# A scan with state followed by an MLP: a new order table, arithmetic taken off GpSimd, and loads issued by two queues

## The chip, the cores and the metric

One core of a Trainium2 chip runs the whole program. The time is microseconds on the device, from one launch, median of three runs.

## The reference, cut to what matters

```python
B, H, S, D = 4, 8, 768, 40                       # r, k, v, w, a, b: [B, H, S, D], float32
state = zeros((B, H, D, D))
for t in range(S):
    y[:, :, t] = einsum('bhd,bhde->bhe', r_t, state)
    Sa = einsum('bhde,bhe->bhd', state, a_t)
    state = state * w_t[:, :, None, :] - einsum('bhd,bhe->bhde', Sa, b_t)
    state = state + einsum('bhd,bhe->bhde', v_t, k_t)
x = y.transpose(0, 2, 1, 3).reshape(3072, 320)
h = x @ w_in                                     # 320 -> 2048
g = h * erf(softplus(h))
out = g @ w_out                                  # 2048 -> 320
```

The state of each of 32 heads is a 40 x 40 matrix that 768 steps of time update one after the other. The MLP needs x, the outputs of all heads of a time step.

## The kernel before, in words

The scan is done in chunks of 32 time steps. Two groups (g) of 16 heads each are gone through one after the other, each in 6 stages of 128 steps, so there are 12 stages (q = 0 to 11) of 4 chunks (c). `build` (L1074) writes the operations of all stages down in program order. Five parts make a stage:

- `prep` (L618): loads w, and builds decay products over the stage by scans on VectorE (scanS L632, scanP L636).
- `aphase` (L645), per chunk: loads k, b and a in one transfer (kba, L666), scales them (ab L667, bk L672), multiplies on TensorE into PSUM (A, L677), masks (Am, L684) and writes the lower part to HBM (AD, L686); transposes b (bT, L695).
- `tphase` (L701), once a stage: reads the triangles of all chunks back (Ti, L711; Ap, L714), solves them on VectorE by 14 pairs of small operations (Tm L724, Ts L725), writes the result out and reads it in another layout (TD L727, tb L730), transposes it (R, L733) and completes the inverse on TensorE (W, DAD, L740).
- `chain` (L750), per chunk, the part that is serial over time: loads of v in two layouts (zv, vx), of r (rt), and of r and v side by side (rv, L771, tile vt); then Zm <- state (L778), Z (L785), zt, U (L794), us (L798), the 4 pieces of u put into the tile Vu (L799 to L806: in stage 0 copies from PSUM named zmu, later 4 transfers a chunk named zu), UT (L821), vtu, PQ (L830), PQm (L833), MY (L841, L845), and the new state (MT, L848) and the output (Ym, L852), which goes to HBM (xw, L858) at the end of a stage.
- the MLP, for 8 blocks of 256 tokens by 256 columns a stage: `load_x` (xr, xh L989, xl L990), mm1 in three-part precision (L1006), hc (copy out of PSUM, L1010), the activation built of tanh, ln, exp and gelu on ScalarE (L1014), nd and rho on VectorE (L1039, L1040), then E and G (L1051, L1052) and mm2 (L1061). The weights arrive as 64-bit floats and are converted in the first part of the run (w1 to w6, wlo, wr1; L932 to L963).

Each operation goes through `Plan.add` (L276) with the list of engines that may run it. What runs where and when is not decided there: `Plan.schedule` (L301) takes two tables, `ORDER` (L16), a permutation of all operations in which a negative number means a filler, and `ENGINES` (L202), one letter for each operation in program order (P TensorE, A ScalarE, V VectorE, G GpSimd, S SyncE). The instructions are emitted in the order of the table; each engine, and SyncE as the only issuer of transfers, works through its own in that order and waits in place. A filler (`warm`, L578) is a 512-column bf16 matmul of a constant that nothing reads. If the lengths don't fit the operations, a list scheduler (L314 on) makes an order instead.

`dma` (L575) puts every transfer on SyncE. The tile vt has 104 rows (two halves of heads, at rows 0 to 39 and 64 to 103) of 8 x 128 columns; one transfer of 104 x 4 KB fills it.

Of the kernel before, what the change touches and what calls it, by code (L numbers as in the profile page):

```python
# [1192 lines left out]
```

## Time and profile before

| | us |
|---|---|
| runs | 860.70, 861.12, 871.73 |
| median | 861.12 |
| span of the profiled execution (first to last instruction) | 855.2 |

The profiled execution's own time is not listed apart from its span; the median is 5.9 us above that span. A page of the profile gives busy times of the engines; the chain of waits follows the work that ended last back from the end; stretches are counted from the start of the span.

### The profile page before, as it was taken

To read this page: it belongs to the slowest core of one execution; us is meant where nothing else is said; L and a number is where in the kernel's file an instruction comes from. 1 tells how busy PE (TensorE), PEld (TensorE's weight loads), DVE (VectorE), ACT (ScalarE), POOL (GpSimd) and SP (SyncE) were. 2 spreads that over 40 slices of the span, in tenths; PEclk is the share of its full clock that TensorE was granted. 3 is DMA by queue.
4 is the path that set the end of the run, shared out by engine and by line. 5 is a ranking of instruction groups with operands and counts; after the bars stand their busy time and mean duration, and the time that the engine had idled before them with its cause. 6 is when DMAs were issued, how large, how long until landed. Compare 5 with 4: busy or idle time off the path is not lost.

```text
span 855.2 us, 32264 instructions
## 1 busy us (share of the span) xinstructions
PE 741.9 (87%) x13794; PEld 572.6 (67%) x13794; DVE 626.0 (73%) x1331; ACT 563.6 (66%) x1055; POOL 145.3 (17%) x124
## 2 busy tenths in 40 slices
PE   0596898798889998989888998899899999899987
PEld 0343546667767777767667776687777777677864
DVE  5588776687767787879687887768688766565764
ACT  5156424677756776865875874685685787567993
POOL 0302111102012012033030100231130240112100
PEclk9998998999999999999999999989999999899998
DMA  7756664665675755556645555746546543512100
GB/s 213 216 155 156 172 157 119 134 135 142 135 169 115 145 139 123 138 121 143 160 122 118 139 130 115 158 109 146 141 112 128 126 112 92 123 39 66 36 16 19
DMA packets 185585, 107.58 MB, mean 126 GB/s; under 512 B 134268, under 2 KB 167804, under 8 KB 185436
## 3 DMA queue, kind: packets, MB, share of 16 engines
q1 hardware_dynamic: 185436, 105.46, 51.8%
q8 instruction: 110, 1.80, 0.9%
q14 instruction: 39, 0.32, 0.1%
HBM read 83.72 MB, written 14.16 MB: 114 GB/s over the span
## 4 chain that ended last, share of the span: by engine, by line
PE 43%; DMA 21%; DVE 14%; SPq 8%; ACT 6%; issue 6%; POOL 1%; DVEq 0%; ACTq 0%; POOLq 0%
PE po L1061 15%; PE ph L1006 10%; SPq L576 8%; DMA Zs<-Ab 3%; PE pA L740 3%; DMA Ti<-AD 3%; PE ph L579 3%; DMA Tb<-TD 2%; PE my L841 2%; PE pQ L830 2%; PE pA L677 2%; DMA bk<-in_kba_e 2%; DMA AD<-Zs 2%; DVE h L1052 2%; PE my L794 2%
## 5 line engine op out<-in xcount | busy, mean ns | idle before, releaser
L1061 PE MATMUL po<-wo,h 128*128 128x320 f32 x768 | 255.1, 459 | 6.1 <-DVE h L1052 5.8
L1061 PEld LDWEIGHTS po<-wo,h 128*128 128x128 f32 x768 | 135.7, 195 | 51.4 <-DVE h L1052 8.7
L1014 ACT ACTIVATE l<-l 128x512 f32<-128x512 f32 x192 | 112.0, 625 | 18.2 <-DVE nd L1039 14.4
L1006 PE MATMUL ph<-xh,wih 128*128 128x256 f32 x384 | 96.1, 332 | 3.4 <-ACT h L571 3.4
L1006 PE MATMUL ph<-xh,wil 128*128 128x256 f32 x384 | 78.0, 285 | 0.0
L1006 PE MATMUL ph<-xl,wih 128*128 128x256 f32 x384 | 77.7, 284 | 0.0
L1052 DVE SCALAR_TENSOR_TENSOR h<-l,h 128x512 f32<-128x512 f32 x96 | 70.3, 739 | 3.0 <-POOL l L1051 2.1
L1040 DVE SCALAR_TENSOR_TENSOR r<-nd,r 128x512 f32<-128x512 f32 x96 | 68.1, 709 | 5.9 <-POOL nd L1039 4.8
L1039 POOL TENSOR_TENSOR nd<-l,r 128x512 f32<-128x512 f32 x27 | 35.7, 1321 | 206.9 <-DVE r L1040 120.4
L1006 PEld LDWEIGHTS ph<-xh,wih 128*128 128x128 f32 x384 | 61.3, 194 | 10.2 <-ACT h L571 4.3
L571 ACT COPY Zm<-MT 40x320 f32<-40x320 f32 x71 | 32.4, 457 | 50.5 <-DVE MT L848 45.6
L579 PE MATMUL ph<-d 104*128 104x512 bf16 x257 | 65.7, 407 | 0.0
L1051 POOL TENSOR_TENSOR l<-l,r 128x512 f32<-128x512 f32 x27 | 38.2, 1419 | 158.6 <-ACT l L1014 85.8
L1006 PEld LDWEIGHTS ph<-xh,wil 128*128 128x128 f32 x384 | 60.6, 194 | 3.9 <-issue 3.9
L1014 ACT ACTIVATE l<-h 128x512 f32<-128x512 f32 x96 | 57.2, 628 | 7.2 <-DVE h L573 6.0
L1006 PEld LDWEIGHTS ph<-xl,wih 128*128 128x128 f32 x384 | 60.2, 192 | 0.0
L1039 DVE TENSOR_TENSOR nd<-l,r 128x512 f32<-128x512 f32 x69 | 49.7, 721 | 11.6 <-ACT r L1014 9.5
L1006 PE MATMUL ph<-xl,wir 128*128 128x256 f32 x192 | 54.9, 286 | 3.8 <-issue 3.7
L841 PE MATMUL my<-Vu,sg 64*40 64x72 f32 x1536 | 48.5, 233 | 8.7 <-DVE h L1052 3.1
L1014 ACT ACTIVATE r<-r 128x512 f32<-128x512 f32 x96 | 55.2, 624 | 0.4
L1014 ACT ACTIVATE r<-l 128x512 f32<-128x512 f32 x96 | 54.2, 619 | 1.5 <-DVE l L1051 1.4
L1006 PE MATMUL ph<-xh,wir 128*128 128x256 f32 x192 | 54.8, 285 | 0.0
(137 smaller groups left out, 1472.5 us busy)
## 6 DMA issues: line engine op xcount, KB each, us to landing
vt<-in_rv_e SPq DMA_DIRECT2D x48, 416.0 KB
bk<-in_kba_e SPq DMA_DIRECT2D x45, 416.0 KB
wo<-in_moe_w_in SPq DMA_DIRECT2D x10, 512.0 KB
h<-in_moe_w_out SPq DMA_DIRECT2D x10, 512.0 KB
Pr<-in_w_e SPq DMA_DIRECT2D x12, 419.7 KB
Rt<-in_r_e SPq DMA_DIRECT2D x48, 104.0 KB
Vu<-in_v_x SPq DMA_DIRECT2D x96, 40.0 KB
Zm<-in_v_s SPq DMA_DIRECT2D x48, 80.0 KB
```

Source lines behind the costliest of these rows:

```text
L571: self.nc.scalar.copy(o, i)
L576: self.P.add(name, "SP", lambda e: self.nc.sync.dma_start(o(), i()), rd, wr, pr, ISSUE.get(name, 0.41))
L579: self.nc.tensor.matmul((self.ph[1], self.pQ)[x], self.d1[:, :128], self.d1[:, :512], start=True, stop=True)
L740: nc.tensor.matmul(pw[js, i], l[js, i], r[js, i], start=True, stop=True)
L841: nc.tensor.matmul(my[h * 64:h * 64 + 40, x, j], sg[xs, j, h], vu[xs, j // 2 * 2 + h, j % 2], start=True, stop=False)
L1006: nc.tensor.matmul(ph[:, j * 256:j * 256 + 256], a[:k, fs], b[:k], start=(m == 0), stop=(m == 7))
L1014: self.P.add(name, "ACT", lambda e: nc.scalar.activation(out=o, in_=i, **kw), rd, wr + ["act"], pr, 0.62)
L1039: P.add("nd", [("DVE", 0.69), ("POOL", 1.28)], lambda e, r=r, l=l, nd=nd: s.eng(e).tensor_tensor(out=nd, in0=l, in1=r, op=ALU.mult), [("l" ...
L1040: P.add("rho", "DVE", lambda e, r=r, nd=nd: nc.vector.scalar_tensor_tensor(out=r, in0=nd, scalar=2 * C4, in1=r, op0=ALU.add, op1=ALU.mult) ...
L1051: P.add("E", [("POOL", 1.28), ("DVE", 0.69)], lambda e: s.eng(e).tensor_tensor(out=l, in0=l, in1=r, op=ALU.mult), [("r", ir)], [("l", il)] ...
L1052: P.add("G", "DVE", lambda e: nc.vector.scalar_tensor_tensor(out=h, in0=l, scalar=-1.0, in1=h, op0=ALU.add, op1=ALU.mult), [("l", il)], [( ...
L1061: nc.tensor.matmul(po, h[:, bs], s.wo[:, f], start=(f == 0), stop=(f == 15))
```

## The change

1. `ORDER` and `ENGINES` are replaced by two others. The list scheduler is removed; where the tables don't fit the operations, program order with the first engine of each list is used.
2. No arithmetic operation lists GpSimd any more: ab, bk, w5, wlo, wr1, xl, MT0, MTs, nd, E have VectorE alone. Only fills with constants at the start are still GpSimd's.
3. Loads (kba, rv, rt, zv, vx, w, wd and constants) may be issued by SyncE or by GpSimd; a sixth letter, Q, in the table says which.
4. The pieces of u (zu) are in all stages an operation that reads the SBUF tile Us, and the table says for each whether it is a transfer by SyncE or a copy by ScalarE or VectorE.
5. rv is loaded as two transfers of 40 rows of 3 KB, one for each half of the heads; the tile vt is filled with zeros once at the start and has another layout (r of half 0 in columns 0 to 255, v and u of both halves in 256 to 767, r of half 1 in 768 to 1023). PQ and vtu read and write it accordingly.
6. In stage 0 the fourth chunk's kba goes to the second bk tile, no longer to a vt tile.

```diff
-    def dma(...): self.P.add(name, "SP", lambda e: self.nc.sync.dma_start(o(), i()), rd, wr, pr, ISSUE.get(name, 0.41))
+        q = {"SP": self.nc.sync, "POOLQ": self.nc.gpsimd}
+        self.P.add(name, [("SP", ISSUE.get(name, 0.41))] + [("POOLQ", 1.0)] * (name in BULK), lambda e: q[e].dma_start(o(), i()), rd, wr, pr)
...
+BULK = ("kba", "rv", "rt", "zv", "vx", "w", "wd", "tri", "ident", "msk")
...
-        P.add("ab", [("POOL", 1.2), ("DVE", 0.69)], ...)
+        P.add("ab", [("DVE", 0.69)], ...)
...
-        s.dma("rv", lambda: vr, lambda: I["rv_e"][g, ck].rearrange("p (a x) -> p a x", a=NP), wr=[("vt", ivt, 0), ("vt", ivt, 1)], pr=prl)
+        for h in range(2):
+            s.dma("rv", lambda h=h: vr[h * 64:h * 64 + 40, h * 256:h * 256 + 768], lambda h=h: I["rv_e"][g, ck, h], wr=[("vt", ivt, h)], pr=prl)
...
-            if q == 0:
-                P.add("zmu", [("ACT", 0.28), ("DVE", 0.32)], lambda e, uv=uv, js=js: s.copy(e, uv, pz[js]), ["pz"], [("vu", iv, "u", j)], pr)
-            else:
-                s.dma("zu", lambda uv=uv: uv, lambda js=js: uo[js], [("us", iu, "-")], [("vu", iv, "u", j)], pr)
+            q2 = {"SP": nc.sync.dma_start, "ACT": nc.scalar.copy, "DVE": nc.vector.tensor_copy}
+            P.add("zu", [("ACT", 0.28), ("DVE", 0.25), ("SP", 0.6)], lambda e, uv=uv, js=js: q2[e](uv, uo[js]), [("us", iu, "-")], [("vu", iv, "u", j)], pr)
...
-                nc.tensor.matmul(pq[...], vr[:, n_, 64:], vr[:, n_, :64].rearrange("p (h t) -> p h t", h=2), start=True, stop=True)
+                nc.tensor.matmul(pq[...], vr[:, 256 + n_ * 64:320 + n_ * 64], vr.rearrange("p (a x) -> p a x", a=4)[:, ::3, n_ * 32:n_ * 32 + 32], start=True, stop=True)
```

What the tables hold, counted by the names of the operations (before | after):

| | before | after |
|---|---|---|
| operations | 4416 | 4466 (48 more for rv, 2 fills of vt) |
| fillers in all | 257 | 141 |
| fillers before the first W, from there to the first mm1, later | 116, 141, 0 | 92, 49, 0 |
| transfers issued by SyncE / GpSimd | 907 / 0 | 654 / 187 |
| of GpSimd's 187 | | vx 58, rv 48, zv 32, rt 18, kba 14, wd 8, w 7, constants 2 |
| zu of stages 1 to 11: SyncE / ScalarE / VectorE | 176 / 0 / 0 | 62 / 87 / 27 |
| arithmetic on GpSimd | nd 27, E 27, xl 20, bk 19, ab 10, w5 8, wr1 2, wlo 1, MTs 1 | none |
| copies on VectorE: hc, Sm (ysM), vt (vtu), sg (bTc) | 20, 21, 16, 10 | 7, 8, 5, 5 |

After the fourth chunk's MY of stage 1, and at the end of each later stage, both tables have placed the same number of mm1 within 3 and of mm2 within 6; TensorE's matmuls are the same in both, fillers apart.

VectorE's list of stage 0, from the last Am of chunk 3 to R (digits count occurrences; Tm, Ts 0 to 13 are the solve of stage 0):

```
before: Am7 Am6 rGc0 w13 w15 w33 w35 scanS1 rG1 w53 wlo1 w17 scanP1 w37 w54 w16 Tm0 Ts0 ... Tm5 wlo3 wlo2
        w55 w36 Ts5 Tm6 Ts6 Tm7 Ts7 w56 w18 bk5 Tm8 Ts8 w38 w19 w39 Tm9 Ts9 ... Tm13 wlo6 Ts13
        w110 w310 w113 wlo4 wlo5 w111 w311 w313 w112 R0
after:  Am7 Am6 w16 w54 w36 scanS1 w17 rG1 w55 w37 scanP1 Tm0 Ts0 Tm1 Ts1 ... Tm13 Ts13
        w56 w110 w18 w19 w38 wlo4 w39 wlo5 w58 w310 w57 ab4 w111 wlo6 w59 R0
```

## Rows read from the trace of the kernel before

**Rows 1.** The page, busy time of each engine in us, share of the span, number of instructions.
```profile
PE 741.9 (87%) x13794; PEld 572.6 (67%) x13794; DVE 626.0 (73%) x1331; ACT 563.6 (66%) x1055; POOL 145.3 (17%) x124
```
**Rows 2.** The page, the chain that ended last: shares of the span by engine, then by line.
```profile
PE 43%; DMA 21%; DVE 14%; SPq 8%; ACT 6%; issue 6%; POOL 1%; DVEq 0%; ACTq 0%; POOLq 0%
PE po L1061 15%; PE ph L1006 10%; SPq L576 8%; DMA Zs<-Ab 3%; PE pA L740 3%; DMA Ti<-AD 3%; PE ph L579 3%; DMA Tb<-TD 2%; PE my L841 2%; PE pQ L830 2%; PE pA L677 2%; DMA bk<-in_kba_e 2%; DMA AD<-Zs 2%; DVE h L1052 2%; PE my L794 2%
```
**Rows 3.** Four stretches of the span, cut at the first W matmul, the end of stage 0's last MY and the end of stage 11's last MY: length, busy us of each engine with its instructions, granted TensorE clock, mean share of the DMA engines, GB/s.
```profile
0.00:75.60 75.60, 37.70 (x233) 19.69 (x234) 51.79 (x107) 33.31 (x63) 14.23 (x18) 0.98 0.67 180
75.60:126.60 51.00, 47.13 (x1017) 27.17 (x1018) 38.25 (x86) 23.08 (x53) 6.51 (x6) 0.96 0.69 177
126.60:789.00 662.40, 598.56 (x12267) 481.73 (x12266) 495.27 (x1073) 457.15 (x859) 119.78 (x98) 0.97 0.54 126
789.00:855.20 66.20, 58.54 (x281) 44.06 (x281) 40.67 (x68) 50.11 (x82) 4.78 (x3) 0.94 0.08 25
```
**Rows 4.** TensorE's timeline from 0 to 145 us: start, length, line, operation, count. L677 is A, L740 W, L841 MY (one piece), L579 a filler, L1006 mm1.
```profile
26.53 1.12 PE L677 MATMUL pA<-T,Pr 104*64 104x64 f32 x16 [1.35 <-issue]
...
75.59 1.93 PE L740 MATMUL pA<-T,Ap 32*32 32x32 f32 x128 [7.87 <-DVE T L733]
...
89.87 0.34 PE L841 MATMUL my<-Vu,sg 64*40 64x72 f32 x8
...
94.31 0.69 PE L677 MATMUL pA<-Ab,bk 104*64 104x64 f32 x16
...
125.41 0.34 PE L841 MATMUL my<-Vu,sg 64*40 64x72 f32 x8
...
126.36 2.55 PE L579 MATMUL ph<-d 104*128 104x512 bf16 x11
...
143.54 0.48 PE L1006 MATMUL ph<-xh,wih 128*128 128x256 f32 x2
```
**Rows 5.** VectorE's timeline from 0 to 80 us, same columns. L684 is Am, L932, L933 and L937 are w1, w3 and w5, L632 and L636 the scans, L724 and L725 the solve, L733 R.
```profile
38.06 0.88 DVE L684 TENSOR_TENSOR Zs<-pA,tri 64x256 f32<-64x256 f32 x2 [1.44 <-PE pA L677]
...
39.05 0.76 DVE L932 TENSOR_SCALAR r<-wo 128x512 int32<-128x512 int32 x2
...
39.73 1.28 DVE L933 SCALAR_TENSOR_TENSOR r<-wo,r 128x512 int32<-128x512 int32 x2
...
45.16 2.36 DVE L632 TENSOR_TENSOR_SCAN Wt<-Pr,d 104x516 f32<-104x516 f32 x2 [4.15 <-ACT Wt L640]
...
50.14 2.35 DVE L636 TENSOR_TENSOR_SCAN Pr<-Pr,d 104x516 f32<-104x516 f32 x2
...
53.21 0.68 DVE L937 TENSOR_TENSOR l<-l,r 128x512 f32<-128x512 f32 x1
...
54.15 0.17 DVE L724 TENSOR_TENSOR tmp<-Ti 128x14 f32<-128x14 f32 x1
...
66.43 0.17 DVE L725 TENSOR_TENSOR Ti<-Ti,tmp 128x14 f32<-128x14 f32 x1
...
74.78 0.71 DVE L733 STREAM_TRANSPOSE T<-Tb 128x512 f32<-128x512 f32 x1
```
**Rows 6.** Groups of instructions by line: count | busy us, mean ns of one | idle time of the engine before them and what ended it.
```profile
L1051 POOL TENSOR_TENSOR l<-l,r 128x512 f32<-128x512 f32 x27 | 38.2, 1419 | 158.6 <-ACT l L1014 85.8 <-DVE r L1040 64.0 <-ACT Us L571 7.5
...
L1039 POOL TENSOR_TENSOR nd<-l,r 128x512 f32<-128x512 f32 x27 | 35.7, 1321 | 206.9 <-DVE r L1040 120.4 <-ACT r L1014 86.5
...
L1039 DVE TENSOR_TENSOR nd<-l,r 128x512 f32<-128x512 f32 x69 | 49.7, 721 | 11.6 <-ACT r L1014 9.5
...
L724 DVE TENSOR_TENSOR tmp<-Ti 128x14 f32<-128x14 f32 (+6 forms) x168 | 35.0, 208 | 13.1 <-DMA Ti<-AD 8.8
...
L573 DVE COPY h<-ph 128x512 f32<-128x512 f32 x20 | 13.6, 684 | 5.2 <-PE ph L1006 3.6 <-PE po L1061 1.5
...
L573 DVE COPY Zm<-MT 40x320 f32<-40x320 f32 x25 | 8.4, 335 | 0.6
...
L573 DVE CAST xh<-xr 128x256 fp32r<-128x256 f32 x19 | 9.3, 492 | 4.0 <-DMA xr<-xd 3.8
```
**Rows 7.** Pieces of the chain that ended last, in order of time: start, length, what.
```profile
46.38 2.81 DMA Ti<-AD
...
398.50 5.05 DMA vt<-in_rv_e
...
459.80 6.62 DMA Ti<-AD
...
827.68 1.27 POOL l L1051
```
**Rows 8.** GpSimd's timeline from 400 to 470 us.
```profile
444.90 1.19 POOL L672 TENSOR_TENSOR bk<-bk,Wt 104x512 f32<-104x512 f32 x1 [2.41 <-DMA bk<-in_kba_e]
```
**Rows 9.** VectorE's timeline from 440 to 462 us.
```profile
445.38 1.26 DVE L667 TENSOR_TENSOR Ab<-bk,Pr 104x512 f32<-104x512 f32 x1 [0.30 <-DMA Zs<-Ab]
```
**Rows 10.** The issuing instructions of SyncE (line 576): ns of one, shortest, median and longest, and first and last start.
```profile
L576 SPq DMA_DIRECT2D Vu<-Us x176: 585/605/1823, 141.2 to 784.4; - x176
```

More of the change, by code (lines that the diff above doesn't have):

```diff
@@ L1 @@
 from contextlib import ExitStack
-import heapq
 import numpy as np
@@ L236 @@
-PARAMS = dict(K=dict(warm=43.6))
+ORDER = tuple(int(x) for x in """
[121 rows of a table added]
+""".split())
+ENGINES = "".join("""
+QSQVVGVGGGGVAAGAGAAAVVGAASAVVVVSVSSVPVVSSPASVSSVPVVSSPASVSSVPVVSSPASVSSVPVVSSPASSSSAAVVVVVVVVVVVVVVVVVVVVVVVVVVVVSSSSVPPPPVPPPPVSVVAAAVAVSVVAAAVAVSVVAAAVAVQVVAAAVAVSVVAAAVAVQVVAAAV
+AVQVVAAAVAVQVVAAAVAVSVVAAAVAAVAVSVVAAAVAAVAVSVVAAAVSVVAAAVQVVAAAVQVVAAAVSVVAAAVQVVAAAVSVVAAAVSVVAAAVQVVAAAVSVVAAAVSAVVVVQVSSVPVVSSPASVSSVPVVSSPASVSSVPVVSSPASVSSVPVVSSPAQQQSQQAVPVPA
+AVAAPAPAPVPVVQQSQSQVAPAPAAAAAPAPAPVPVVQSQQSSAAPAPAAAAAPAPAPVPVVSQSQSSAAPAPAAAVAPAPAPVPVVSSSSSSSSAAVVVVVVVVVVVVVVVVVVVVVVVVVVVVSSSSVPPPPVPPPPVSVVSAVSSVVPPAAPPAAPPAAPPAAAAAAAAAAAAAAA
@@ L237 @@
+PPPPPPAAVVPPPPVVPPPPVSVSAAAAAAAAAAAAAAVVVVVVVVAAAAAPPVAPPAAVVPPPPPPAAVVPPPPPPVAVVPPPPVVPPPPAAAAAAAAAAAAAAVVVVVVVVAAAAAVVPPPPVVPPPPVVPPPPVVPPPPASAS
+""".split())
+PARAMS = dict()
 L, C, NP = 128, 32, 8
@@ L244, with __init__ @@
 LSC = -(0.5 - 2.0 ** -24)
-TICK = 10.24 / 3
-FETCH, BLOCK, PHASE = 3.6, 127.3, 94.9
-PAIRS = dict(W=32, DAD=32, mm1=8, mm2=2, A=16, PQ=16, Z=32, U=32, MY=64, pmt=4, UT=2, bT=4, cT=1)
-COLS = dict(W=1024, DAD=1024, mm1=2048, mm2=1280, A=1024, PQ=1024, Z=1280, U=1280, MY=3328, pmt=416, UT=256, bT=416)
-HOLD = dict(zu=0.08, rt=0.2, vx=0.12, tri=0.09, msk=0.09, Ap=0.37, ident=0.18, w=1.19, kba=1.2, nr=1.82, zv=0.23, rv=1.3, zs=0.12, AD=0.37, Ti=0.73, TD=0.73, tb=0.37, xw=0.23, xr=0.28, out=0.46, wd=0.73)
-ISSUE = dict(zs=0.83, Ti=0.58, TD=0.58, xr=0.62, tb=0.49, Ap=0.49)
-FREE = ("Am", "PQm", "MT", "Ym", "zt", "zmu", "us", "vtu", "ysM", "bTc", "ob", "hc", "Wm", "Tb", "zgb", "zcb")
-TAIL = dict(UT=0.22, pmt=0.18, bT=0.19, mm1=0.16, mm2=0.15, cT=0.15)
-class Plan:
-    BANKS = ("pA", "pQ", "pQb", "pz", "my", ("ph", 0), ("ph", 1), ("po", 0), ("po", 1))
-    SPARE = (("ph", 1), "pQ")
-    HOP = {"PE": 0.05, "ACT": 0.04, "DVE": 0.04, "POOL": 0.04, "SP": 1.6}
-    OVL = {"PE": 0.0, "ACT": 0.1, "DVE": 0.08, "POOL": 0.04, "SP": -0.09}
-    def __init__(self, offset={}, filler=None, since=0.0, only={}, order=(), engines=""):
+ISSUE = dict(zs=0.83, Ti=0.53, TD=0.53, xr=0.6, tb=0.64, Ap=0.64, vx=0.6, zu=0.6)
+BULK = ("kba", "rv", "rt", "zv", "vx", "w", "wd", "tri", "ident", "msk")
+CODE = dict(P="PE", A="ACT", V="DVE", G="POOL", S="SP", Q="POOLQ")
+class Plan:
+    def __init__(self, filler=None, order=(), engines=""):
         self.ops = []
         self.order, self.engines = order, engines
-        self.offset, self.only = offset, only
-        self.filler, self.since, self.tag = filler, since, ""
+        self.filler, self.tag = filler, ""
         self.wr, self.rd = {}, {}
     def add(self, name, eng, fn, rd=(), wr=(), pr=0, dur=None):
-        if pr != -1e3:
-            pr += self.offset.get(name + self.tag, self.offset.get(name, 0.0))
         alts = eng if isinstance(eng, list) else [(eng, dur)]
-        alts = [(e, d, e == "POOL" or e == "DVE" and name not in FREE) for e, d in alts]
         i = len(self.ops)
@@ L295, in add @@
             self.rd[k] = []
-        every, one = alts, self.only.get(name + self.tag, self.only.get(name))
-        alts = [x for x in every if x[0] == one] or every
-        self.ops.append(dict(name=name, tag=self.tag, alts=alts, all=every, fn=fn, deps=deps, pr=pr, banks=[k for k in rd if k in self.BANKS], uses=[k for k in self.SPARE if k in rd or k in wr]))
+        self.ops.append(dict(name=name, tag=self.tag, alts=alts, fn=fn, deps=deps, keys=set(rd) | set(wr)))
         return i
     def schedule(self):
-        ops = self.ops
@@ L303, in schedule @@
-        n = len(ops)
-        if len(self.engines) == n and sorted(x for x in self.order if x >= 0) == list(range(n)):
-            for o, e in zip(ops, self.engines):
-                o["eng"] = dict(P="PE", A="ACT", V="DVE", G="POOL", S="SP")[e]
-            out = []
-            for x in self.order:
-                if x < 0:
-                    ops.append(dict(name="warm", eng="PE", fn=lambda e, x=-1 - x: self.filler(x)))
-                    x = len(ops) - 1
-                out.append(x)
-            return out
@@ L314, in schedule @@
-        succ = [[] for _ in range(n)]
-        left = [0] * n
-        for i, o in enumerate(ops):
-            left[i] = len(o["deps"])
-            for d, raw in sorted(o["deps"]):
-                succ[d].append((i, raw))
-        ready_at = [0.0] * n
-        free = {e: 0.0 for e in self.HOP}
-        ticks = {}
-        queue = lock = 0.0
-        only = [o["alts"][0][0] if len(o["alts"]) == 1 else "" for o in ops]
-        bank = {k: ("", 0.0) for k in self.BANKS}
-        uses = {k: sum(k in o["uses"] for o in ops) for k in self.SPARE}
@@ L328, in schedule @@
-        used = {k: 0 for k in self.SPARE}
-        last = {k: 0.0 for k in self.SPARE}
-        fetch = [0.0, PHASE]
-        def clocked(now, d, cols, pairs=1):
-            k = int(now / TICK)
-            if ticks.get(k - 1, 0.0) < 3300:
-                d *= 2
-            if pairs >= fetch[1]:
-                t = now + d * fetch[1] / pairs
-                d += max(0.0, fetch[0] + FETCH - t)
-                fetch[0] = max(t, fetch[0] + FETCH)
-                fetch[1] += BLOCK
-            fetch[1] -= pairs
-            x = now
-            while x < now + d - 1e-9:
-                k = int(x / TICK + 1e-9)
-                y = min(now + d, (k + 1) * TICK)
-                ticks[k] = ticks.get(k, 0.0) + cols * (y - x) / d
-                x = y
-            return d
@@ L352, in schedule @@
-        pend = [(0.0, i) for i in range(n) if not left[i]]
-        heapq.heapify(pend)
-        avail = []
-        start = [0.0] * n
-        now = 0.0
-        done = 0
-        key = lambda i: (ops[i]["pr"], i)
-        while done < n:
-            while pend and pend[0][0] <= now + 1e-9:
-                t, i = heapq.heappop(pend)
-                avail.append(i)
-            avail.sort(key=key)
-            rest = []
-            for i in avail:
-                o = ops[i]
-                best = None
-                for e, d, k in o["alts"]:
-                    if k and lock > now + 1e-9:
-                        continue
-                    if any(bank[k][0] != e and bank[k][1] > now + 1e-9 for k in o["banks"]):
-                        continue
-                    if free[e] <= now + 1e-9 and (best is None or d < best[1]):
-                        best = (e, d, k)
-                if best is None:
-                    rest.append(i)
-                    continue
-                e, d, k = best
-                occ = max(d - self.OVL[e], 0.05)
-                if e == "PE":
-                    occ = clocked(now, d, COLS.get(o["name"], 0), PAIRS.get(o["name"], 1))
-                    d = occ + TAIL.get(o["name"], 0.07)
-                o["eng"], start[i] = e, now
-                o["start"], o["end"] = now, now + d
-                free[e] = now + occ
-                if k:
-                    lock = now + occ
-                done += 1
-                for k in o["uses"]:
-                    used[k] += 1
-                    last[k] = max(last[k], now + d)
-                for k in o["banks"]:
-                    bank[k] = (e, now + d + self.HOP[e])
-                if e == "SP":
-                    queue = max(now + d + 0.58, queue) + HOLD[o["name"]]
-                fin = queue if e == "SP" else now + d
-                for j, raw in succ[i]:
-                    if only[j] == e and e != "SP" and (e == "PE" or not raw):
-                        t = now + occ
-                    else:
-                        t = fin + (0.1 if only[j] == "POOL" and e != "SP" else self.HOP[e])
-                    ready_at[j] = max(ready_at[j], t)
-                    left[j] -= 1
-                    if not left[j]:
-                        heapq.heappush(pend, (ready_at[j], j))
-            avail = rest
-            if self.filler and free["PE"] <= now + 1e-9 and ticks.get(int(now / TICK), 0.0) < 6800 and now >= self.since:
-                spare = [x for x, k in enumerate(self.SPARE) if (used[k] == 0 if x == 0 else used[k] == uses[k] and last[k] <= now)]
-                if spare:
-                    d = clocked(now, 0.214, 512)
-                    free["PE"] = now + d
-                    ops.append(dict(name="warm", eng="PE", fn=lambda e, x=spare[0]: self.filler(x), start=now, end=now + d, deps=()))
-                    start.append(now)
-            nxt = [f for f in list(free.values()) + [lock] + [b[1] for b in bank.values()] if f > now + 1e-9]
-            if pend:
-                nxt.append(pend[0][0])
-            if not nxt:
-                break
-            now = max(now + 1e-6, min(nxt))
@@ L420, in schedule @@
-        assert done == n, (done, n)
-        self.total = max(o["end"] for o in ops)
-        return sorted(range(len(ops)), key=lambda i: (start[i], i))
+        ops, n = self.ops, len(self.ops)
+        if len(self.engines) != n or sorted(x for x in self.order if x >= 0) != list(range(n)):
+            for o in ops:
+                o["eng"] = o["alts"][0][0]
+            return list(range(n))
+        for o, e in zip(ops, self.engines):
+            o["eng"] = CODE[e]
+        out = []
+        for x in self.order:
+            if x < 0:
+                ops.append(dict(name="warm", eng="PE", fn=lambda e, x=-1 - x: self.filler(x)))
+                x = len(ops) - 1
+            out.append(x)
@@ L425, in restride @@
+        return out
 def restride(ap, dim, step):
@@ L462, in host @@
     o["r_e"] = stk(re).reshape(NG, 24, 104, NP * 32)
-    rv = np.zeros((NG, 24, 104, NP, 4, 32), np.float32)
-    rv[..., :2, :] = diag(el(r)).transpose(0, 1, 2, 4, 3, 5)
-    rv[..., 2, :] = stk(el(v))
-    o["rv_e"] = np.ascontiguousarray(rv[:, :, :, [pair(n) for n in range(NP)]]).reshape(NG, 24, 104, NP * 128)
+    rs, vs = [el(x)[:, :, :, :, [pair(n) for n in range(NP)]] for x in (r, v)]
+    vu = np.zeros((NG, 24, 2, 40, NP, 2, 32), np.float32)
+    vu[..., 0, :] = vs
+    rv = np.zeros((NG, 24, 2, 40, 3 * NP * 32), np.float32)
+    for h in range(2):
+        rv[:, :, h, :, (256, 0)[h]:(768, 512)[h]] = vu[:, :, h].reshape(NG, 24, 40, NP * 64)
+        rv[:, :, h, :, (0, 512)[h]:(256, 768)[h]] = rs[:, :, h].reshape(NG, 24, 40, NP * 32)
+    o["rv_e"] = rv
     vs = v.reshape(NG, NB, 4, 2, 24, 32, 40).transpose(0, 4, 5, 1, 2, 3, 6)
@@ L500, in __init__ @@
         K = self.K
-        self.P = Plan(K.get("po", {}), self.warm, K.get("warm", 4.0), order=ORDER, engines=ENGINES)
+        self.P = Plan(self.warm, ORDER, ENGINES)
         pool = lambda n, **k: ctx.enter_context(tc.tile_pool(name=n, bufs=1, **k))
```

105 lines of the change are left out of this document (42 added, 63 removed), and 305 rows, old and new, of the table ORDER.

## The prediction, made before the changed kernel was run

> **What bounds the kernel now.** I read the page's busy shares first, then the chain of waits by engine, then the stretches, and last the timelines of the places where a stretch is idle. No engine fills the span: TensorE 87%, VectorE 73%, ScalarE 66% [rows 1]. In the chain that ended last TensorE holds 43%, transfers 21%, VectorE 14%, and SyncE's own issuing (SPq) 8% [rows 2]. So the kernel is bound by a chain that changes engines, not by one engine. The stretches split it in four [rows 3]. Up to the first W matmul (75.6 us) TensorE does almost nothing but the dependency-free filler matmuls. From there to the end of stage 0 (51.0 us) it is busy 47.13 us, but much of that is fillers again. The middle, 126.6 to 789.0, holds eleven stages of 60.2 us (662.4 / 11), and TensorE is idle 662.4 - 598.6 = 63.8 us of it. The last 66.2 us is the MLP of what is left. The head, 143.5 us until the first MLP matmul [rows 4], and the idle of the middle are where an order can win; the tail is a chain of its own.
>
> **Head: the order of VectorE's work.** In the table of before, VectorE ends the last A-phase multiply of stage 0 (Am) at 38.94 and starts the transpose R at 74.78, 35.8 us later [rows 5]. Between lie stage 1's scan, the 28 small operations of the triangular solve, spread over 54.15 to 66.6 (12.4 us), and many operations on the weights. In the new table there stand between Am and the solve only six weight operations (two each of w1, w3, w5: 0.38, 0.64 and 0.68 us by [rows 5], 3.4 us) and stage 1's two scans with the reciprocal (2.4 + 2.4 + about 0.4 us): 8.6 us; then the 28 small ones in one piece, 28 x 0.208 = 5.8 us [rows 6]. From the last of them to R the transfers out and back and what VectorE does meanwhile took 74.78 - 66.6 = 8.2 us, which I leave. That makes 22.6 us instead of 35.8. What could still hold the solve is the way of A through HBM: Ti lands at 46.38 + 2.81 = 49.2 [rows 7], 10.3 us after Am, later than the 8.6 above. With it, and 0.7 us for ScalarE's two fills, the sum is 11.0 + 5.8 + 8.2 = 25.0. Gain between 10.8 and 13.2; I take 12.
>
> **Head: fillers.** The old list has 257 fillers, the new one 141. From the first W to the first mm1 they are 141 and 49. Eleven of them took 2.55 us between two real matmuls [rows 4], 0.23 us each, so 92 fewer free 21 us of TensorE. Not all of it is on the path: from the first to the fourth MY the old run needs 35.5 us [rows 4]. VectorE's own operations in that stretch of the new table add up to about 25 us by the durations of their lines and cannot shrink. So at most 35.5 - 25 = 10.5 is there; I take 8, and 2 for the stretch from W to the first MY, which loses 17 fillers (4 us). The cover lost is TensorE's pace: an A took 1.12 us at 26.5, when TensorE had mostly stood idle, and 0.69 at 94.3, among fillers [rows 4]. If the thinner filling brings the slow pace back, 12 us of matmuls in these steps cost up to 12 x (1.12 / 0.69 - 1) = 7 us more; that stays in the range. **Head in sum: 12 + 8 + 2 = 22 us** (bounds 10 and 24).
>
> **No arithmetic on GpSimd.** GpSimd is busy 145.3 us with 124 instructions [rows 1], nearly all arithmetic, 1.3 to 1.4 us for what VectorE does in 0.72 [rows 6]. All 115 operations of that kind move to VectorE: 143 x 721 / 1321 = 78 us more there. VectorE gives back 13 hc copies (13 x 0.684 = 9 us) and 29 other copies (about 14 us, between [rows 6]'s 0.335 and 0.684 each) to ScalarE and takes 27 zu copies (at 0.335, 9 us): 78 - 9 - 14 + 9 = 64, so 690 us. Of a span of 812 that is 85%, no bound yet. And part of the 145 us was VectorE's already: while GpSimd held bk from 444.90 to 446.09 [rows 8], VectorE's Ab needed 1.26 us [rows 9] instead of 0.68. On the chain GpSimd has 1%, 8.6 us; at half the duration that is 4 us saved. The load added to VectorE is hidden behind TensorE as long as it has 15% free. If that cover goes, it costs by VectorE's share of the chain: 14% of 855 = 120 us, times 64 / 626, 12 us. I take 3 of these 12, since the chain has more TensorE than VectorE in it, and as much goes from the collisions.
>
> **Transfers.** SyncE issues 907 transfers before and 654 after; 187 go to GpSimd's queue. Of the 176 zu transfers of stages 1 to 11 (0.605 us of issue each [rows 10]) 62 stay on SyncE; 114 become copies of 0.3 us on ScalarE (87) and VectorE (27). ScalarE gets some 45 us with hc and the other copies, 564 + 45 = 609, 75% of the new span. Everything still on SyncE stands behind 28% fewer issues. SPq is 8% of the chain, 68 us [rows 2]; 28% of that is 19 us. The rv load is cut from 104 rows of 4 KB to 2 x 40 rows of 3 KB, 8.4 MB of 105 MB less. DMA engines are busy 54% of the middle [rows 3], so I cost that at nothing; where rv is on the chain it shows 5.05 us [rows 7], and a few such places are what it could give. No row shows a transfer issued by GpSimd: its price lies between nothing (these are loads, wanted later) and the case of the third rival below. I take nothing, as GpSimd has no other work left.
>
> **Sum.** Middle: 4 + 19 - 3 = 20 us of the 63.8 idle, 1.8 per stage (bounds 0 and 45, leaving TensorE 97% busy). Tail: the same operations; the last E on GpSimd, 1.27 us [rows 7], becomes VectorE's at 0.7: 1 us with its hand-over. 855.2 - 22 - 20 - 1 = **812 us of span**; the median lies 861.1 - 855.2 = 5.9 us above this span (the page gives no own time for the profiled execution), so **818 us**.
>
> **The rivals.**
> *Only the head moves.* If VectorE's 64 us and ScalarE's 45 us eat what SyncE gives, the middle stays at 60.2 us a stage: 861 - 23 = 838, or 841 where the head gives 20. For it: VectorE and ScalarE get fuller in every stage. Against: they have 15 and 25% free.
> *The middle opens further.* Ti landed 2.81 us after its first issue in the head and 6.62 in the middle, behind the bulk loads issued just before it [rows 7]. Ti and Tb are 5% of the chain, 43 us [rows 2]. If bulk loads on a queue of their own stop delaying them, (6.62 - 2.81) / 6.62 = 58% of that goes, 25 us: 818 - 25 = 793, and with the head's upper bound 791. The Trainium skill ("DMA: Bandwidth & Descriptors", Issuing engines are not separate DMA queues) says that transfers from all engines interleave on the same 16 DMA engines, and that several issuers save only issue time. By it this rival falls away and the 818 stands. No run here shows two issuers.
> *Loads from GpSimd come late (slower).* Each of 48 steps needs zv, vx, rv before its matmuls, and TensorE waits in order. If they come d late in each, the cost is 48 d; from d = 0.9 us the gains of 43 us are gone, from (43 + 17) / 48 = 1.25 us the kernel is slower by over 2%; at 1.5 us it is 818 + 72 = 890. For it: no row shows how long such an issue takes, and 48 rv, 58 vx and 32 zv go there. Against: the loads have buffers of two in rt, vt and vu. The Trainium skill ("SBUF — State Buffer", Who interferes with whom) gives a cause: a GpSimd-issued transfer cannot write its descriptors while VectorE copies in a two-port mode. VectorE's copies within SBUF, Zm and xh, are 17.7 us [rows 6], 2% of the span, so by the rule an issue in fifty is held for 0.5 us, and that alone does not reach 0.9.
> *It does nothing to the time*, within 2%: head gain at its lower bound 10 and a middle that loses it, 855. That the table is not taken at all (a fallback to program order) is excluded: it holds 4466 operations, which is the old 4416 plus 48 for rv and 2 fills.
>
> **How the numbers follow.** A measurement of this kernel tells about 2%, 17 us, so faster means below 844. Forecast with its own spread 806 to 830: 0.50; only the head 0.16; further opening 0.16; nothing 0.11; late loads 0.07. Only-the-head is partly inside 2%, so faster 0.80, same 0.13, slower 0.07. The range goes from the opened middle, taken down to 786 because TensorE's busy time holds pipeline ends that closer packing hides, up to 848, above the head-only case; it leaves out the late loads and most of "nothing".
>
> **What would show it.** Right: R of stage 0 near 60 to 64, the first mm1 between 118 and 126; stages of 57 to 60 us; VectorE near 690, ScalarE near 609, GpSimd under 10 us busy; SPq well under 8% of the chain; fillers 141. Wrong: R still after 70; waits of PQ, MY or Z on loads from GpSimd; an A of 1.1 us still after the first MY; VectorE the largest share of the chain.

## The result and the profile after

The changed kernel took 804.0 us (median of 4 runs, 801.5 to 805.0) beside 860.9 for the kernel before on the same chip: a ratio of 0.936 [0.932, 0.941]. That is 57 us less; the forecast was 818 (786 to 848) and faster. The profiled execution has a span of 802.3 us, 52.9 below that of before. Some executions of a kernel are over 1.5% longer at a lower granted clock; medians here include them, ratios and their intervals leave them out.

First the page of after: busy time of each engine with its share and its instructions, then the chain that ended last by engine and by line.

```profile
PE 720.9 (90%) x13678; PEld 570.4 (71%) x13678; DVE 646.2 (81%) x1428; ACT 613.3 (76%) x1187; POOL 108.4 (14%) x199
...
PE 71%; DVE 9%; ACT 6%; DMA 5%; issue 5%; SPq 1%; DVEq 0%; ACTq 0%
PE po L866 23%; PE ph L811 19%; PE pA L546 4%; PE pA L483 4%; PE my L646 3%; PE pQ L635 3%; PE my L601 2%; PE ph L387 2%; ACT r L819 2%; PE my L592 2%; PE pA L501 2%; PE pQ L617 2%; DMA TD<-Ti 2%; PE my L650 1%; PE pQ L626 1%
```

Against [rows 1, 2] the chain has changed its nature: TensorE holds 71% of it instead of 43%, transfers 5% instead of 21%, SyncE's issuing 1% instead of 8%. GpSimd's 108.4 us are no arithmetic: the page counts its transfer issues as busy (see the last section).

The four stretches of after, cut at the same four events as [rows 3], columns as there:

```profile
0.00:58.40 58.40, 28.64 (x208) 14.46 (x209) 51.45 (x107) 35.83 (x67) 13.29 (x29) 0.92 0.85 229
58.40:109.00 50.60, 42.36 (x938) 27.23 (x939) 35.87 (x86) 27.22 (x65) 7.39 (x13) 0.67 0.62 159
109.00:734.90 625.90, 592.76 (x12249) 484.13 (x12246) 515.62 (x1163) 499.72 (x976) 87.68 (x157) 0.97 0.49 117
734.90:802.30 67.40, 57.13 (x293) 44.55 (x288) 43.23 (x74) 50.48 (x82) 0.00 (x0) 0.96 0.08 25
```

Up to the first W 17.2 us went, in the rest of stage 0 0.4, in the eleven stages of the middle 36.5 (60.2 to 56.9 us each; TensorE's idle there falls from 63.8 to 33.1), and the tail took 1.2 more. The second row's granted clock is 0.67, where before had 0.96.

TensorE's timeline of after, 0 to 140 us (L483 is A, L546 W, L646 MY, L811 mm1):

```profile
58.43 1.93 PE L546 MATMUL pA<-T,Ap 32*32 32x32 f32 x128 [12.04 <-DMA Ap<-AD]
...
72.05 1.12 PE L483 MATMUL pA<-Ab,bk 104*64 104x64 f32 x16
75.18 0.48 PE L646 MATMUL my<-Vu,sg 64*40 64x72 f32 x8
...
107.30 0.48 PE L646 MATMUL my<-Vu,sg 64*40 64x72 f32 x8
...
121.01 1.12 PE L483 MATMUL pA<-Ab,bk 104*64 104x64 f32 x16
...
128.13 0.50 PE L811 MATMUL ph<-xh,wih 128*128 128x256 f32 x2
```

VectorE's timeline of after, 0 to 75 us (L490 is Am, L445 the copy that ends scanP, L530 and L531 the solve, L539 R), and from ScalarE's the fill of the solve's tile Ti:

```profile
32.08 0.88 DVE L490 TENSOR_TENSOR Zs<-pA,tri 64x256 f32<-64x256 f32 x2 [0.29 <-PE pA L483]
...
40.78 0.18 DVE L445 COPY Pr<-Wt 104x8 f32<-104x8 f32 x1
40.86 0.17 DVE L530 TENSOR_TENSOR tmp<-Ti 128x14 f32<-128x14 f32 x1
...
47.23 0.18 DVE L531 TENSOR_TENSOR Ti<-Ti,tmp 128x14 f32<-128x14 f32 x1
...
57.50 0.71 DVE L539 STREAM_TRANSPOSE T<-Tb 128x512 f32<-128x512 f32 x1 [0.25 <-DMA Tb<-TD]
```

```profile
40.19 0.55 ACT L524 ACTIVATE Ti<-cst 128x272 f32<-128x272 f32 x2 [1.05 <-DMA Ti<-AD]
```

The last Am ends at 32.96 (38.94 in [rows 5]) and R starts at 57.50 (74.78): 24.5 us between them where there were 35.8. The solve stands in one piece from 40.86 to 47.41. From the last Am to the solve VectorE has no idle time; ScalarE's fill, which had waited for Ti to land, ends at 40.74, 0.1 us before the solve starts.

### The profile page after: what moved, and what is told of

It reads as the page before. It is cut to its first block, busy times and chain, and to the rows that moved or that the text cites. A ratio compares the mean times of both kernels' runs of the same rounds, so it can differ in the third digit from the quotient of the medians.

```text
span 802.3 us, 32141 instructions
## 1 busy us (share of the span) xinstructions
PE 720.9 (90%) x13678; PEld 570.4 (71%) x13678; DVE 646.2 (81%) x1428; ACT 613.3 (76%) x1187; POOL 108.4 (14%) x199
## 3 DMA queue, kind: packets, MB, share of 16 engines
q1 hardware_dynamic: 142489, 68.45, 35.8%
HBM read 75.07 MB, written 14.16 MB: 111 GB/s over the span
## 4 chain that ended last, share of the span: by engine, by line
PE 71%; DVE 9%; ACT 6%; DMA 5%; issue 5%; SPq 1%; DVEq 0%; ACTq 0%
PE po L866 23%; PE ph L811 19%; PE pA L546 4%; PE pA L483 4%; PE my L646 3%; PE pQ L635 3%; PE my L601 2%; PE ph L387 2%; ACT r L819 2%; PE my L592 2%; PE pA L501 2%; PE pQ L617 2%; DMA TD<-Ti 2%; PE my L650 1%; PE pQ L626 1%
## 5 line engine op out<-in xcount | busy, mean ns | idle before, releaser
L866 PE MATMUL po<-wo,h 128*128 128x320 f32 x768 | 273.6, 465 | 7.5 <-DVE flag L680 4.4
L866 PEld LDWEIGHTS po<-wo,h 128*128 128x128 f32 x768 | 128.9, 194 | 40.3 <-issue 5.1
L811 PE MATMUL ph<-xh,wih 128*128 128x256 f32 x384 | 118.8, 391 | 1.4 <-ACT h L378 1.4
L811 PEld LDWEIGHTS ph<-xh,wih 128*128 128x128 f32 x384 | 71.4, 192 | 28.5 <-ACT h L378 2.0
L844 DVE TENSOR_TENSOR nd<-l,r 128x512 f32<-128x512 f32 x96 | 66.0, 688 | 16.5 <-ACT r L819 12.5
L811 PE MATMUL ph<-xl,wih 128*128 128x256 f32 x384 | 77.7, 284 | 0.0
L811 PE MATMUL ph<-xh,wil 128*128 128x256 f32 x384 | 77.5, 284 | 0.0
L378 ACT COPY h<-ph 128x512 f32<-128x512 f32 x89 | 51.3, 580 | 23.0 <-PE ph L811 22.0
L856 DVE TENSOR_TENSOR l<-l,r 128x512 f32<-128x512 f32 x96 | 64.9, 683 | 1.0 <-ACT l L819 0.2
L811 PEld LDWEIGHTS ph<-xh,wil 128*128 128x128 f32 x384 | 60.2, 192 | 0.0
L811 PEld LDWEIGHTS ph<-xl,wih 128*128 128x128 f32 x384 | 59.9, 192 | 0.0
L490 DVE TENSOR_TENSOR Zs<-pA,tri 64x256 f32<-64x256 f32 x96 | 40.6, 423 | 22.5 <-PE pA L483 20.1
L811 PE MATMUL ph<-xl,wir 128*128 128x256 f32 x192 | 54.6, 285 | 0.0
L811 PE MATMUL ph<-xh,wir 128*128 128x256 f32 x192 | 54.5, 284 | 0.0
L384 POOL DMA_DIRECT2D Vu<-in_v_x x58 | 34.8, 601 | 140.3 <-PE my L650 137.3
L483 PE MATMUL pA<-Ab,bk 104*64 104x64 f32 x720 | 34.2, 241 | 19.5 <-DVE bk L478 15.9
```

Source lines behind the costliest of these rows:

```text
L378: self.nc.scalar.copy(o, i)
L384: self.P.add(name, [("SP", ISSUE.get(name, 0.41))] + [("POOLQ", 1.0)] * (name in BULK), lambda e: q[e].dma_start(o(), i()), rd, wr, pr)
L483: nc.tensor.matmul(pa[i % 2 * 64:i % 2 * 64 + 64, i // 4, i // 2 % 2], bk[:, i].rearrange("p a b -> p (a b)"), ab[:, :, i], start=True, st ...
L490: P.add("Am", "DVE", lambda e, x=x, xs=xs: nc.vector.tensor_tensor(out=zx[64:128, x], in0=pz[xs], in1=s.tri[xs, None, :].to_broadcast([64, ...
L811: nc.tensor.matmul(ph[:, j * 256:j * 256 + 256], a[:k, fs], b[:k], start=(m == 0), stop=(m == 7))
L844: P.add("nd", [("DVE", 0.69)], lambda e, r=r, l=l, nd=nd: s.eng(e).tensor_tensor(out=nd, in0=l, in1=r, op=ALU.mult), [("l", il), ("r", ir) ...
```

## The experiments

Three groups, each on one chip with the kernel before beside it. Ratios are to that; two kernels of different groups are compared by their ratios.

**First group: which part of the middle carries the gain** (before: 860.6).

*All transfers back on SyncE's queue* (the 187 that GpSimd issues), order and engines kept:

```
-            o["eng"] = CODE[e]
+            o["eng"] = CODE["S" if e == "Q" else e]
```

> The changed kernel, its order and engines kept, but the 187 transfers of GpSimd are issued by SyncE at the same places of the order. Theory Q (the second queue and the emptier SyncE open the middle): the time goes up by 15 us or more, 819 to 835, and SPq and transfers come back onto the chain from 1% and 5%. Rival O (the order alone brought the gain, the issuer hardly matters): within 5 us of 804.

Measured 800.1, ratio 0.933 [0.928, 0.938], against 0.936 [0.932, 0.941] with two issuers. The chain of waits of this kernel, by engine:

```profile
PE 68%; DVE 9%; DMA 7%; ACT 6%; issue 5%; SPq 2%; DVEq 0%; ACTq 0%
```

This is rival O's outcome. SPq is 2% with every transfer on SyncE, as in a second execution of the changed kernel (the control below). The second issuer is worth nothing here that can be measured, and it was not what took SyncE off the chain.

*The pieces of u of stages 1 to 11 as transfers again* (114 copies on ScalarE and VectorE become SyncE transfers):

```
+            o["eng"] = "SP" if o["name"] == "zu" and o["tag"] != "_0" else CODE[e]
```

> The changed kernel with all zu of stages 1 to 11 as transfers by SyncE (114 copies of ScalarE and VectorE become transfers, all else kept). Theory Q: 114 x 0.6 us = 69 us more issuing on SyncE and a transfer's latency instead of a copy before MY: 10 to 25 us slower, 814 to 829. Rival O: within 5 us, as ScalarE and VectorE get 34 us back.

Measured 900.2, ratio 1.052 [1.044, 1.059]: 96 us above the changed kernel, slower than before, and far outside both expectations. Its chain by engine and by line, and then the largest waits for u (engine, line, tile, waited for: us in all, times, longest):

```profile
PE 51%; DMA 16%; DVE 11%; issue 7%; ACT 7%; SPq 6%; DVEq 0%; ACTq 0%; POOLq 0%
PE po L866 16%; PE ph L811 14%; DMA Vu<-Us 8%; PE pA L546 4%; PE my L646 3%; SPq L384 3%; SPq L611 3%; ACT r L819 2%; PE pA L483 2%; PE my L601 2%; PE my L592 2%; PE pQ L617 2%; DMA Ti<-AD 2%; DMA Tb<-TD 1%; PE pQ L635 1%
```

```profile
DVE MT L653 <- PE my L650: 57.8, 27, 4.4
...
ACT Zm L378 <- DVE MT L653: 47.8, 20, 4.8
PE my L646 <- DMA Vu<-Us: 47.1, 26, 3.7
```

One such step from its chain (start, length, what):

```profile
333.48 0.38 SPq L384
...
333.92 1.49 SPq L611
...
336.79 0.59 SPq L611
...
337.43 4.33 DMA Vu<-Us
341.76 0.14 issue
341.89 0.48 PE my L646 x5
```

And the pieces as copies in the changed kernel, stage 0's 16 among them (operation, count: ns at least/median/most):

```profile
L611 ACT COPY Vu<-Us x101: 320/323/327, 70.4 to 731.1; 32x160 f32<-32x160 f32 x101
...
L611 DVE COPY Vu<-Us x29: 232/235/241, 71.6 to 731.8; 32x160 f32<-32x160 f32 x29
```

MY waits for u in 26 places, and VectorE (MT) and ScalarE (Zm) wait behind it: one late tile is handed on through three engines. In the changed kernel MT's and Zm's waits are 6.7 and 14.0 us, and MY waits for no transfer of u. A copy of 0.24 to 0.32 us stands where a transfer takes an issue of 0.59 and 4.33 us to land; and in the step shown 3.3 us of SyncE's other issues, from 333.48 on, stand on the chain ahead of it. So the way and the queue both count: the way has 8% of this chain, SyncE's issuing 6%, half of it for other transfers. The middle grew by 86 us, from 626.0 to 711.6: TensorE is idle for 57 of them, and for 28 it is busy longer, at a granted clock of 0.94 where the changed kernel has 0.97.

*The 115 operations back on GpSimd*, at their new places (GP lists name and occurrence of those that had been there):

```
+            k = seen[o["name"]] = seen.get(o["name"], -1) + 1
+            o["eng"] = "POOL" if k in GP.get(o["name"], ()) else CODE[e]
```

> The changed kernel with the 115 arithmetic operations that GpSimd had before back on GpSimd, at the places of the new order. Theory P (arithmetic on GpSimd costs by its length, by blocking VectorE and by holding the loads queued behind it): 15 to 40 us slower, 819 to 844. Rival V (VectorE is the tight engine now and gains 75 us of air): same or faster, 795 to 806.

Measured 817.5, ratio 0.951 [0.945, 0.957]: 13.5 us slower than the changed kernel, just less than theory P expected. Its busy times, two lines of its VectorE (operation, count, busy us, mean ns, idle before), then the same two in the changed kernel:

```profile
PE 728.2 (89%) x13678; PEld 573.1 (70%) x13678; DVE 638.1 (78%) x1313; ACT 613.0 (75%) x1187; POOL 249.1 (31%) x314
```

```profile
L848 DVE SCALAR_TENSOR_TENSOR r<-nd,r 128x512 f32<-128x512 f32 x96 | 70.4, 733 | 14.4 <-POOL nd L847 13.6
...
L847 DVE TENSOR_TENSOR nd<-l,r 128x512 f32<-128x512 f32 x69 | 54.8, 794 | 15.1 <-ACT r L822 11.8 <-DVE r L848 0.5
```

```profile
L844 DVE TENSOR_TENSOR nd<-l,r 128x512 f32<-128x512 f32 x96 | 66.0, 688 | 16.5 <-ACT r L819 12.5
...
L845 DVE SCALAR_TENSOR_TENSOR r<-nd,r 128x512 f32<-128x512 f32 x96 | 65.6, 684 | 1.0
```

VectorE is busy 638 us without the 115 operations and 646 with them: they add 8 us, because others become shorter in the mean when GpSimd does no arithmetic beside them (nd 794 to 688 ns, r 733 to 684). It is those that meet GpSimd's: of the 69 nd on VectorE here, the 13 that overlap an arithmetic operation of GpSimd by more than 0.1 us take 1.25 us in the mean, the other 56 take 0.69. And VectorE no longer stands 13.6 us waiting for GpSimd's nd.

*The same 115 operations to VectorE in the order of before*:

```
+                o["eng"] = "DVE" if e == "G" and o["name"] in ("ab", "bk", "w5", "wlo", "wr1", "xl", "MTs", "nd", "E") else dict(P="PE", A="ACT", V="DVE", G="POOL", S="SP")[e]
```

> The kernel before, its order kept, with the same 115 operations on VectorE instead of GpSimd. Theory P: 3 to 15 us faster, 846 to 858. Rival V (VectorE's 64 us more cost where nothing is reordered): 865 to 875. My prediction had 1 us in favour (4 gained, 3 lost).

Measured 865.0, ratio 1.011 [1.004, 1.017]: 1% slower, at the edge of what rival V expected. VectorE is busy 664.2 us, 38 more than before, and has 22% of the chain instead of 14%. The edit that is worth 13 us in the new order costs a little in the old one.

**Second group: copies, engine table, bytes, fillers** (before: 865.0).

*Only the pieces of u as copies, in the order of before* (the string ZU holds the new table's choice for each of the 176):

```
+            zu = iter(ZU)
-                s.dma("zu", lambda uv=uv: uv, lambda js=js: uo[js], [("us", iu, "-")], [("vu", iv, "u", j)], pr)
+                P.add("zu", "SP", lambda e, uv=uv, js=js: q2[e](uv, uo[js]), [("us", iu, "-")], [("vu", iv, "u", j)], pr, 0.41)
```

> The kernel before, its order and all else kept, with the 114 pieces of u that the new table copies (87 ScalarE, 27 VectorE) as copies instead of transfers. Theory Z (the copies are worth their 96 us, found the other way round in the new order, in any order): 800 to 840. Rival L (the old order had other work placed under these transfers, the new one has not; the copies are worth only what SyncE gets back): 840 to 860.

Measured 873.9, ratio 1.011 [1.007, 1.016]. My theory (copies pay by themselves) fell, and the loss was larger than the rival allowed. The old order hid the transfers of u: they have 8 us of the chain of before, and MY waited for them twice. For the copies it waits longer (line of before, then two of this kernel):

```profile
PE my L841 <- DMA Vu<-Us: 1.6, 2, 1.2
```

```profile
PE my L844 <- ACT Vu L809: 7.7, 5, 2.8
...
PE my L844 <- DVE Vu L809: 4.6, 5, 1.9
```

A copy is short but waits its turn on its engine: it starts 1.8 us (ScalarE) and 3.9 us (VectorE) after u is in Us, in the median, against 1.3 and 1.1 in the changed kernel.

*The whole new engine table in the old order*, all transfers on SyncE (the diff is the string ENGINES alone):

```
-    "SSSVVGVGVGAAAVVGAGVVVAASAVVVVSVSSVPVVSSPVSGSSVPVVSSPASVSSGPVVSSPASVSSVPVVSSPASSSSAAVVV
+    "SSSVVGVGGGGVAAGAGAVVGAASAVVVVSVSSVPVVSSPASVSSVPVVSSPASVSSVPVVSSPASVSSVPVVSSPASSSSAAVVV
...
```

> The order of before with the whole engine table of the new kernel (no arithmetic on GpSimd, 114 copies of u, the other copies moved to ScalarE), all transfers on SyncE. What is left to the new kernel with all transfers on SyncE (800) is the order, the fillers and the split of rv. Theory Z: at or below 830. Rival L: 840 to 865, the order is the larger part and the engines pay only with it.

Measured 904.9, ratio 1.036 [1.026, 1.047], slower than both expectations. No trace of it is read here. By the ratio the engine table alone costs about 32 us. With the new order, its fillers and the cut load (the first kernel of the first group) the ratio is 0.933: these are worth 0.10 of 861, some 89 us, with this table.

*The bytes of rv put back* (each half loads 64 or 40 rows of 4 KB in place of 40 rows of 3 KB; by the pages 83.72 MB read from HBM in place of 75.07, so 8.65 MB more), run again with the third group:

```
-            s.dma("rv", lambda h=h: vr[h * 64:h * 64 + 40, h * 256:h * 256 + 768], lambda h=h: I["rv_e"][g, ck, h], wr=[("vt", ivt, h)], pr=prl)
+            s.dma("rv", lambda h=h: vr[(0, 64)[h]:(64, 104)[h]], lambda h=h: I["rv_e"][g, ck, (0, 64)[h]:(64, 104)[h]], wr=[("vt", ivt, h)], pr=prl)
```

> The changed kernel with rv's two transfers widened to 64 and 40 rows of 4 KB, so that the bytes are those of before (8.4 MB more), number and places kept. The prediction's step (hidden, costs nothing): within 5 us of 804. Rival (bandwidth counts): 5 to 15 us slower.

> The widened rv loads (8.4 MB more) again, with the control on the same chip. If the bytes count as the first run suggests: 10 to 18 us over the control. The prediction's step: within 5 us of it.

Measured 822.2, ratio 0.952 [0.944, 0.960], and the second time 816.3, 0.950 [0.945, 0.954], 11.9 us above the changed kernel in the same group (804.4). The wider loads cost about 1.5%, as the rival expected. All of it lies in the middle: the last MY of stage 11 in the changed kernel run beside it, and in this one,

```profile
734.25 0.33 PE L646 MATMUL my<-Vu,sg 64*40 64x72 f32 x7
```

```profile
745.55 0.33 PE L646 MATMUL my<-Vu,sg 64*40 64x72 f32 x7
```

while stage 0 ends at 113.0 and 112.8. Of these 11.3 us TensorE is idle for 4, and for 7 it is busy longer, at a granted clock of 0.96 instead of 0.97. Why 240 KB in place of 416 KB a step are worth 0.26 us a step (11.3 / 44 steps), with the DMA engines half busy, the traces don't say.

*52 more fillers ahead of the first W*, to fill the 12 us in which TensorE stands still:

```
+i = ORDER.index(118)
+ORDER = ORDER[:i] + (-1,) * 52 + ORDER[i:]
```

> The changed kernel with 52 more fillers right before the first W, where TensorE stands idle for 12 us and then goes on at half its pace up to 80 us. Theory C (the idle stretch costs the pace of the matmuls behind it): first MY 2 to 4 us earlier, 1 to 4 us of the whole. Rival: the head is bound by VectorE, no change, or up to 2 us slower if the fillers end after Ap has landed.

Measured 792.5, ratio 0.914 [0.907, 0.921], the changed kernel having 0.936: some 19 us, where 1 to 4 were expected. The first MY, which was to come earlier, started at 76.39 instead of 75.18, and stage 0 ends at 112.8 (109.0 in the changed kernel, 113.0 in its control): the gain is not the one that I had in mind. It lies in the middle, which takes 613.5 us (625.9 and 621.7).

**Third group: the fillers again** (before: 858.4).

*The changed kernel itself, as the control*:

> The changed kernel itself again, on the chip of the next three, as their control: 800 to 812.

Measured 804.4, ratio 0.937 [0.932, 0.942].

*26 more fillers* (the edit above with 26):

> The changed kernel with 26 instead of 52 more fillers right before the first W. The 52 gained some 12 us, but not in the head: the first MY came 1 us later, and the gain lay behind 500 us, where stalls of TensorE for which the profile shows no wait were gone. Theory S (these stalls come at places that the number of TensorE's instructions ahead of them decides): a time of its own, anywhere from 788 to 812, with the stalls of over 0.9 us at other places than in either. Rival C (warmth of the head): between the control and the 52.

Measured 787.0, ratio 0.917 [0.912, 0.921]: 17.4 us below the control, the fastest version of all, and below both expectations. Two stretches of the control, then of this kernel, cut at the same times; columns as in [rows 3]:

```profile
58.00:109.00 51.00, 40.34 (x862) 26.30 (x864) 35.47 (x84) 24.75 (x59) 7.39 (x13) 0.63 0.58 154
109.00:727.00 618.00, 585.46 (x12154) 478.77 (x12153) 510.49 (x1156) 497.80 (x973) 87.25 (x157) 0.97 0.49 119
```

```profile
58.00:109.00 51.00, 39.19 (x943) 24.80 (x944) 38.60 (x92) 27.91 (x67) 7.39 (x13) 0.78 0.64 166
109.00:727.00 618.00, 595.45 (x12281) 488.76 (x12282) 520.17 (x1171) 505.46 (x985) 86.91 (x157) 0.97 0.49 120
```

From 58 to 109 us the granted clock is 0.78 instead of 0.63, and the last MY of stage 0 ends at 107.0 instead of 113.0. Of the 15.0 us between the two profiled executions these are 6.0; the other 8.9 lie in the middle, at an equal granted clock. There TensorE is idle for 22.7 us instead of 32.5. It has stalls to which the trace gives no releaser ("issue"), at W above all; in TensorE's largest waits, the control and then this kernel:

```profile
PE pA L546 <- issue: 14.2, 8, 5.4
```

```profile
PE pA L548 <- issue: 4.2, 3, 2.6
```

After 120 us the stalls of this kind longer than 0.9 us sum to 20.2 us in the control and 6.2 here; the last section says what they are.

*52 fillers with all transfers on SyncE*:

> The changed kernel with all transfers on SyncE and the 52 fillers. If both gains (some 4 and 12 us) are separate: 784 to 792. If the fillers' gain is an accident of places: 792 to 806.

Measured 792.2, ratio 0.923 [0.919, 0.926]. The two edits don't add up, and 52 are no better than 26.

## Why the prediction held, and where it did not

Sign, size and range held, but the number came near by errors that cancel, and that is luck: of the terms only the issuer's and, in sum, the one from Am to R came true.

**The head, Am to R: right in sum, by parts that cancel.** I said 25.0 us between the last Am and R; it is 24.5. The sum had 11.0 up to the solve, 5.8 for it and 8.2 from there to R; the trace has 7.9, 6.6 and 10.1. The 11.0 was the way of A through HBM, which I took to outlast VectorE's own 8.6. It did not: VectorE works without a pause up to the solve, and the fill that waits for Ti ends 0.1 us before it. R itself is earlier than the 60 to 64 that I gave, since the last Am ends 6.0 us earlier (32.96), which no term of mine had.

**The head, fillers: wrong.** This step charged the 92 fillers left out as 8 + 2 us gained from W to the fourth MY. From W to the first MY the kernel lost 2.4 (14.3 to 16.75), from there to the fourth it gained 3.4 (35.5 to 32.1): 1.0 in place of 10. What failed is in the step's own bound, the cover that I named and priced at up to 7 us but left in the range: TensorE stood still for 12.04 us before W, the granted clock of that stretch is 0.67 (so a good part of it at the lower of the two levels, 1.2 and 2.4 GHz), and the A at 72.05 takes 1.12 us where [rows 4] has 0.69. The run with 26 more fillers, at 0.78 there, ends the stretch 6 us earlier than the control. So the first mm1 came at 128.1, just past the 126 that I had allowed, and a sign of being wrong that I had named came true: an A still takes 1.12 us at 121.01, after the first MY. The head's sum is 17.6 us against 22, and 6.0 of the 17.6 are the earlier Am. Even that is soft: in the control, the same kernel, stage 0 ends at 113.0 and not 109.0, and stage 11 still within a microsecond of where it did; 4 us at that point are not 4 us at the end.

**The middle: right in sign, the price wrong.** I gave 20 us, 19 of them from SyncE's queue. It is 36.5, at 56.9 us a stage. SyncE did leave the chain (8% to 1%), so the sign that I had named came true, but the price does not hold. With all 841 transfers on SyncE's queue the time is the same and SPq 2%; so the split over two queues gives nothing. And the count of issues doesn't give the time: the 114 pieces of u as copies save 114 issues in the old order and make the kernel 1.1% slower, while in the new order taking them out costs 96 us. There SyncE's issuing does come back, to 6% of the chain, but the transfer's way has more, 8%, and the sum had no term for it: 4.33 us behind the issue in the piece shown against 0.32 for a copy, in a chain from U over MY and MT to Zm. In the old order the same transfers were hidden: from the end of us, the copy of u into Us, to the first MY of its chunk there are 6.2 us in the median (4.6 at least) in the kernel before, and 4.9 (2.9) in the changed one. So what the change brings is the pair: an order in which u is wanted sooner, and engines that deliver it sooner. Each alone is a loss: the engine table in the old order has the ratio 1.036, the new order without the copies 1.052. That it is the order that draws these steps together is read from the traces; no run moves single steps of the order, or puts the whole old engine table into the new one.

**No arithmetic on GpSimd: right that it gains, sizes off.** VectorE is at 646 us and not 690, because the price of 78 us for the moved operations leaves out how much shorter others get; the pairs of kernels above put it at 8 us in the new order and 38 in the old. I had 1 us for this edit and what it loads on VectorE; it is 13.5, by the run that puts the operations back. In the old order it is worth nothing (ratio 1.011). ScalarE at 613 us is as said (609).

**The rv load at nothing: wrong.** "DMA engines are busy 54%" was no reason that fewer bytes are free: the narrower loads are worth about 12 us (and are 8.65 MB less, not 8.4). My own bound, the few places with 5.05 us of vt on the chain, was the better number.

**The tail**: +1.2 in place of -1. **GpSimd as issuer at nothing**: right.

**The rivals.** The range's lower part, "the middle opens further" (791 to 793), came nearer in time, not by its mechanism: it wanted bulk loads on a queue of their own to stop delaying Ti and Tb, and a second queue gives nothing. Ti and Tb did leave the chain, 46.6 us before and 15.5 after, but no less with one queue (12.7). The Trainium skill ("DMA: Bandwidth & Descriptors", Issuing engines are not separate DMA queues) says that transfers of all issuers share the same DMA engines; 800 with one issuer and 804 with two agree with it. "Loads from GpSimd come late" falls with the same pair: TensorE's nine largest waits in the changed kernel name no load of zv, vx or rv, and its chain has 9.4 us of zv's loads where the kernel before has 8.5. "Only the head moves" and "nothing" fall with the middle's 36.5.

The forecast was 14 us too high. It had 4 too much for the head and 2 for the tail, and 16 too little for the middle: that makes 10. By the runs that take one part out, GpSimd's arithmetic is worth 12 more than I gave and rv 12 more; what is left for the 19 of SyncE can't be had by taking these off, since the parts don't add up. The other 4 are the way from span to median, 1.7 us here (804.0 - 802.3) where I took 5.9, the median of some executions less the span of another.

## What to carry to other kernels

An order and an engine table that were searched together are one change: parts of it tried in the old order each cost 1 to 4%, so price the pair by what the new order wants next, and test by taking a part out of the new kernel, not by putting it into the old one. Before a transfer is priced by its issue, look in the chain whether its landing stands there; before an operation is priced on its new engine, ask what it did to its neighbours on the old one. And where filler matmuls are thinned out, put the slower pace of what follows into the sum, not into the range. Where a stall has no releaser, look whether the queue that loads instructions was at work.
